# Attention with keys split 3 x 128 + 64, and attention-times-V in four 64x64 tiles, inside a fused attention and FFN kernel

## Chip, cores and metric

The kernel runs on one core of one Trainium2 chip. The metric is the device time of one execution in microseconds (us). Where two kernels are compared, runs from the same chip and the same rounds are used, all of them in the fast state. The experiments ran on four chips, each with the kernel before beside them, so runs of different groups are to be compared by their ratio to it. Times within a run, such as the first `xn`, come from the one execution whose trace was kept. A single core has only one span, so "state" here only says that a run lies within 1.5% of the fastest of its kernel.

Engines are named as in the profile: PE is TensorE's matmuls, PEld its weight loads, DVE is VectorE, ACT is ScalarE, POOL is GpSimd, SP is SyncE. `L179` is line 179 of the kernel. "Half clock" is a stretch in which the trace records a granted TensorE clock of 0.5.

## The reference, cut

```python
# q, k, v: (8, 12, 448, 64) float32       batch, heads, sequence, head size
scores = q @ k.T / sqrt(64)
attn   = maximum(scores, 0) ** 2 / 448
x      = (attn @ v), heads side by side   # (3584, 768)
xn     = x / sqrt(mean(x * x) + 1e-6) * rms_g
g, val = xn @ w_gate, xn @ w_val          # (768, 1536) each
out    = (silu(g) * val) @ w_out          # (1536, 768)
```

## The kernel before

Eight batches of 448 tokens run through attention and FFN. The attention of batch b+1 is woven, piece by piece, into the FFN matmuls of batch b. That makes *stages*: stage b is the FFN of batch b with the attention of batch b+1 inside. By "batch 1's stage" I mean the first of them, in which batch 1's attention runs. The attention of batch 0 has no FFN to hide in and stands alone at the **start**; I take the start to end with the first `xn` instruction of batch 0, which produces the first input of the FFN.

The heads go in pairs (`j`), one head per half of the partitions. The keys are cut into four chunks of 112. For each pair and chunk, two matmuls make scores with keys on partitions, a relu copies them out of PSUM, and a square follows:

```python
NCH = 4                                     # chunks, PC = 112 keys each
def relu_on(b, j, c):   return "dve" if c == 3 and (b or j % 2) else "act"
def square_on(b, j, c): return "pool" if b == 0 and j >= 3 and c == 1 else "dve"

def scores(b, j, c):
    psS = ps_s.tile([P, 2, 512], FP32, ...)  # ps_s has two buffers
    for hh in range(2):                      # two row halves of the array: 64x128 tiles
        nc.tensor.matmul(out=psS[:, hh, :S], lhsT=<chunk c of k>, rhs=<q>, ...)
    ...                                      # relu into r; the square is queued
```

Attention times V is done for two pairs in one *visit*: 16 matmuls of 112 keys onto 64 columns, two heads side by side (`112*64` in the profile):

```python
def attend(b, j):
    psAV = ps_s.tile([P, 2, 512], FP32, ...)
    for jj in range(2):
        for c in range(NCH):
            for hh in range(2):
                nc.tensor.matmul(out=psAV[hh * D : (hh + 1) * D, jj, :S],
                    lhsT=ld["v", b][:, 2 * (j + jj) + hh, c * D : (c + 1) * D],
                    rhs=rsq[b, j + jj, c][:, hh, :], start=(c == 0), stop=(c == NCH - 1))
    ...                                      # ACT copies psAV to xT
```

The order of one batch's attention. Batches 0 and 1 transpose q and k on PE (`transposes`), later ones by DMA. `keep_busy(n)` runs n matmuls of zeros whose result nobody reads; the kernel before has them at the start.

```python
if b < PE_T:                                 # PE_T = 2
    add(0.4, lambda: transposes(b, 0))
for j in range(HP):                          # 6 pairs
    for c in range(NCH):
        if c == 1 and j in (2, 4):
            add(1.6, lambda j=j: attend(b, j - 2))
        add(0.3, lambda j=j, c=c: scores(b, j, c))
        if c == 1 and b < PE_T and j + 1 < HP:
            add(0.4, lambda j=j: transposes(b, j + 1))
        if b == 0 and c % 2:
            add(0.3, lambda: keep_busy(2))
...
add(1.6, lambda: attend(b, HP - 2), flush)
```

## Time and profile before

| | before |
|---|---|
| median time | 468.93 us (468.92 to 469.4) |
| span in the trace, mean granted clock | 467.2 us, 0.997 |
| end of the start (first `xn`) | 39.75 us |
| first relu | 8.70 us |
| first `xn` of batch 0 to first `xn` of batch 7 (seven stages) | 370.13 us |
| the rest, to the end | 57.32 us |

From the overview page: engine busy time and share, then the span in 40 slices of 11.7 us each (each digit is tenths; `PEclk` is the granted TensorE clock), then the chain of waits.

```profile
PE 455.1 (97%) x5440; PEld 297.1 (64%) x5440; DVE 283.0 (61%) x425; ACT 255.6 (55%) x384; POOL 55.7 (12%) x48
...
PE   7889999999999999999999999999999999999995
...
PEclk9999999999999999999999999999999999999998
DMA  9999999799909930499009950428002200020013
...
PE 92%; DVE 4%; ACT 3%; issue 0%; DVEq 0%
```

PE is the limit nearly everywhere. Two other things matter later: the first three PE digits are lower than the rest, which is the start, and `PEclk` stays at 9 there. DMA is busy at 90% or more for almost all of the first 100 us.

The groups that the change touches (line, engine, operation, tiles, shapes, count; busy time, mean ns of one; idle time before them and what ended it):

```profile
L190 ACT ACTIVATE r<-psS 112x896 bf16<-112x896 f32 x147 | 132.7, 920 | 53.5 <-PE psS L179 52.6
...
L179 PE MATMUL psS<-qkT 64*128 64x448 bf16 x384 | 77.7, 350 | 3.8 <-ACT r L190 3.0
...
L203 PE MATMUL psAV<-r,vb 112*64 112x448 bf16 x384 | 41.3, 355 | 0.9 <-DVE r L188 0.5
```

350 ns is the length of one pipelined matmul, not its cost. The cost is the spacing of starts: inside a visit, the pairs of matmuls start every 0.189 us. I call that a *slot*.

The timeline (start, length, engine, line, operation, tiles, count, idle before it and its releaser): first the beginning of the start, then its end, then one visit.

```profile
8.30 0.55 PE L179 MATMUL psS<-qkT 64*128 64x448 bf16 x4 [0.72 <-DVE qkT L160]
8.70 4.96 ACT L190 ACTIVATE r<-psS 112x896 bf16<-112x896 f32 x6 [6.47 <-PE psS L179]
8.78 0.39 PE L155 MATMUL psT<-ident,kb 112*64 112x112 bf16 x8
...
39.75 3.66 DVE L364 SCALAR_TENSOR_TENSOR xn<-xT,g_sb,rstd 128x448 bf16<-128x448 bf16 x6
...
162.02 1.70 PE L203 MATMUL psAV<-r,vb 112*64 112x448 bf16 x16
163.66 0.36 PE L317 MATMUL psP<-xn,wg_sb 64*128 64x448 bf16 x1
```

The scores of pair 0 start at 8.30 us, *before* the transposes of pair 1 (8.78 us), so ACT begins at 8.70 us. The visit's 8 slots last 1.54 us (8 times 0.189, and 0.02 more in the first); with the 0.09 us on entering and 0.10 us on leaving, in which no slot begins, the visit takes 1.73 us from the end of the slot before it to the start of the matmul after it. Every steady visit takes that, within 2 ns.

### The profile page before, as it was taken

The page shows a single profiled execution, that of the slowest core. Times are in us where ns is not written, and L with a number is a line of the kernel's source. Part 1 is how long each engine was busy: PE and PEld are TensorE (multiplying, and loading weights), DVE is VectorE, ACT ScalarE, POOL GpSimd, SP SyncE. Part 2 cuts the span into 40 slices and gives each one's busy share as a digit, 9 for nine tenths or more (in the row PEclk, how much of TensorE's full clock was granted, in tenths as well). Part 3 has the DMA queues.
Part 4 walks back from the last instruction along what each step waited for, and adds up shares of the span by engine and source line. Part 5 has one row for each costly group of instructions (what it writes and reads, how often), then busy time and mean ns, then how long its engine had stood idle before and what let it go on. Part 6 is the DMA issues. An engine that isn't in the chain of part 4 may idle for free.

```text
span 467.2 us, 12220 instructions
## 1 busy us (share of the span) xinstructions
PE 455.1 (97%) x5440; PEld 297.1 (64%) x5440; DVE 283.0 (61%) x425; ACT 255.6 (55%) x384; POOL 55.7 (12%) x48
## 2 busy tenths in 40 slices
PE   7889999999999999999999999999999999999995
PEld 3335556676667666676667666676667766676674
DVE  2876488687664876397666676587565686442210
ACT  3862366666555766475645766565545766532221
POOL 8355100411004000400004000000000000000000
PEclk9999999999999999999999999999999999999998
DMA  9999999799909930499009950428002200020013
GB/s 107 199 204 199 208 169 135 97 201 142 124 6 169 198 65 0 60 204 138 1 1 138 204 95 1 60 84 139 1 1 67 72 2 0 3 80 24 1 38 99
DMA packets 128052, 43.65 MB, mean 93 GB/s; under 512 B 100608, under 2 KB 124416, under 8 KB 128000
## 3 DMA queue, kind: packets, MB, share of 16 engines
q0 software_dynamic: 88944, 23.60, 52.6%
q1 hardware_dynamic: 39056, 19.28, 21.7%
q8 instruction: 42, 0.69, 0.6%
q14 instruction: 10, 0.08, 0.1%
HBM read 47.19 MB, written 11.01 MB: 125 GB/s over the span
## 4 chain that ended last, share of the span: by engine, by line
PE 92%; DVE 4%; ACT 3%; issue 0%; DVEq 0%
PE psP L317 47%; PE psO L317 23%; PE psAV L203 8%; PE psS L179 7%; PE psB L120 2%; PE psSS L317 2%; ACT r L190 2%; DVE r L188 1%; PE psT L155 1%; DVE r L193 1%; DVE xn L364 1%; PE psP L378 1%; DVE rstd L361 1%; ACT xT L214 0%; DVE qkT L160 0%
## 5 line engine op out<-in xcount | busy, mean ns | idle before, releaser
L317 PE MATMUL psP<-xn,wv_sb 64*128 64x448 bf16 x1140 | 236.1, 349 | 0.0
L317 PE MATMUL psP<-xn,wg_sb 64*128 64x448 bf16 x1128 | 234.1, 349 | 0.1
L190 ACT ACTIVATE r<-psS 112x896 bf16<-112x896 f32 x147 | 132.7, 920 | 53.5 <-PE psS L179 52.6
L317 PE MATMUL psO<-wo_sb,hT 64*128 64x256 bf16 x2016 | 141.2, 270 | 0.0
L317 PEld LDWEIGHTS <-hT 64*128 64x128 bf16 x2016 | 103.3, 94 | 30.3 <-issue 3.1
L317 PEld LDWEIGHTS <-wv_sb 64*128 64x128 bf16 x1140 | 94.9, 94 | 41.5 <-issue 2.7
L193 DVE TENSOR_TENSOR r<-r 112x896 bf16<-112x896 bf16 x189 | 113.6, 624 | 9.7 <-ACT r L190 9.0
L317 PEld LDWEIGHTS <-wg_sb 64*128 64x128 bf16 x1128 | 94.5, 94 | 38.5 <-issue 3.2
L393 DVE TENSOR_TENSOR hT<-sil,psP 128x448 bf16<-128x448 bf16 x96 | 59.5, 619 | 81.8 <-PE psP L317 72.8
L388 ACT ACTIVATE sil<-psP 128x448 bf16<-128x448 f32 x96 | 51.9, 541 | 62.1 <-PE psP L317 55.9
L179 PE MATMUL psS<-qkT 64*128 64x448 bf16 x384 | 77.7, 350 | 3.8 <-ACT r L190 3.0
L188 DVE TENSOR_SCALAR r<-psS 112x896 bf16<-112x896 f32 x45 | 49.0, 1089 | 14.6 <-PE psS L179 13.9
L427 ACT COPY ost<-psO 128x256 f32<-128x256 f32 x84 | 30.8, 372 | 42.9 <-PE psO L317 38.8
L214 ACT ACTIVATE xT<-psAV 128x896 bf16<-128x896 f32 x24 | 22.0, 917 | 41.4 <-PE psAV L203 40.2
L203 PE MATMUL psAV<-r,vb 112*64 112x448 bf16 x384 | 41.3, 355 | 0.9 <-DVE r L188 0.5
L361 DVE RECIPROCAL rstd<-rstd 128x448 f32<-128x448 f32 x8 | 23.6, 2952 | 24.4 <-ACT rstd L357 24.4
L179 PEld LDWEIGHTS <-qkT 64*128 64x128 bf16 x384 | 26.5, 94 | 18.5 <-issue 11.0
L203 PEld LDWEIGHTS <-vb 112*64 112x64 bf16 x384 | 20.5, 109 | 19.1 <-issue 8.5
L364 DVE SCALAR_TENSOR_TENSOR xn<-xT,g_sb,rstd 128x448 bf16<-128x448 bf16 x48 | 29.3, 679 | 0.3
L74 POOL DMA_DIRECT2D vb<-in_v_dram x9 | 8.7, 969 | 173.7 <-PE psAV L203 92.0
L216 DVE TENSOR_TENSOR x<-xT 128x896 bf16<-128x896 bf16 x24 | 14.9, 622 | 23.6 <-ACT xT L214 23.6
L76 POOL DMA_DIRECT2D qb<-in_q_dram x6 | 13.8, 2308 | 45.0 <-DMA qkT<-qb 38.4
(35 smaller groups left out, 145.0 us busy)
## 6 DMA issues: line engine op xcount, KB each, us to landing
qb<-in_q_dram POOLq DMA_DIRECT2D x7, 672.0 KB, 13.0
kb<-in_k_dram POOLq DMA_DIRECT2D x7, 672.0 KB, 17.9
vb<-in_v_dram POOLq DMA_DIRECT2D x7, 672.0 KB, 9.0
out_dram<-ost SPq DMA_DIRECT2D x8, 336.0 KB, 3.2
wg_sb<-in_moe_w_gate_dram POOLq DMA_DIRECT2D x4, 576.0 KB, 18.2
wv_sb<-in_moe_w_val_dram POOLq DMA_DIRECT2D x4, 576.0 KB, 19.8
wo_sb<-in_moe_w_out_dram POOLq DMA_DIRECT2D x2, 1152.0 KB, 24.3
out_dram<-ost SPq DMA_DIRECT2D x8, 288.0 KB, 4.5
```

Source lines behind the costliest of these rows:

```text
L179: nc.tensor.matmul(out=psS[:, hh, :S], lhsT=qkT[b][prt, j].rearrange("p t s -> p (t s)")[:, c * PC : c * PC + P], rhs=qkT[b][prt, j, 1, :] ...
L188: nc.vector.tensor_relu(out=r[:], in_=psS[:PC, :, :S])
L190: nc.scalar.activation(out=r[:], in_=psS[:PC, :, :S], func=ACT.Relu)
L193: pending.append(lambda: eng.tensor_tensor(out=r[:], in0=r[:], in1=r[:], op=ALU.mult))
L203: nc.tensor.matmul(out=psAV[hh * D : (hh + 1) * D, jj, :S], lhsT=ld["v", b][:, 2 * (j + jj) + hh, c * D : (c + 1) * D], rhs=rsq[b, j + jj, ...
L214: nc.scalar.mul(out=xT, in_=psAV[:, :, :S], mul=inv_attn)
L317: mm = nc.tensor.matmul(out=self.ps[:, : self.w], lhsT=self.lhsT(i)[prt], rhs=self.rhs(i)[prt], start=(half == 0 and i == 0), stop=(half = ...
L361: nc.vector.reciprocal(out=rstd[:], in_=rstd[:])
L364: nc.vector.scalar_tensor_tensor(out=xn[:, kt, :], in0=xTs[b][:, kt, :], scalar=g_sb[:, kt : kt + 1], in1=rstd[:], op0=ALU.mult, op1=ALU.mult,
L388: nc.scalar.activation(out=s[:], in_=psG[:], func=ACT.Silu)
L393: nc.vector.tensor_tensor(out=hTs[b // 2][:, fb, o : o + S], in0=sil[b, fb][:], in1=psV[:], op=ALU.mult)
L427: nc.scalar.copy(out=ost[:, o : o + w], in_=ps[:, :w])
```

## The change

The intent is to use PE's array fully. A chunk of 112 keys fills 112 of the 128 rows of the largest tile in the profile (128*128, L120's fillers); three chunks of 128 fill them, and the remaining 64 keys of two head pairs share one slot in four 64x64 tiles. Attention times V is cut to 64x64 as well: each chunk of 128 is two halves of 64 keys, so a visit has 28 matmuls, four at a time. Counted in slots, a batch drops from 24 to 21 for the scores and from 24 to 21 for attention times V.

The core of the diff (loading and the split of `scores` cut):

```diff
     def relu_on(b, j, c):
-        return "dve" if c == 3 and (b or j % 2) else "act"
+        return "dve" if c == UH - 1 or (b and j % 2 and c == 2) else "act"
...
+    def rest_scores(b, j):
+        psS = ps_s.tile([P, 2, 512], FP32, name="psS", tag="psS")
+        for hh in range(2):
+            prt = slice(hh * D, (hh + 1) * D)
+            for jj in range(2):
+                nc.tensor.matmul(
+                    out=psS[jj * D : (jj + 1) * D, hh, :S],
+                    lhsT=qkT[b][prt, j + jj, 0, (UH - 1) * P : (UH - 1) * P + D],
+                    rhs=qkT[b][prt, j + jj, 1, :], start=True, stop=True)
...
-    def attend(b, j):
+    def attend(b, j, then=None):
...
+        def run(first):
+            for step in range(UH - (not first)):
+                for prt, jj in ((low, 0), (high, 1)) if first else ((low, 1), (high, 0)):
+                    r, u = pairs[prt][jj][step]
+                    for hh in range(2):
+                        if not first and step == 0:
+                            tc.add_manual_dep(nc.tensor.nop().ins, last[jj, hh].name, behind)
+                        mm = nc.tensor.matmul(out=psAV[hh * D : (hh + 1) * D, jj, :S],
+                            lhsT=v[prt, 2 * (j + jj) + hh, u * D : (u + 1) * D], rhs=r[prt, hh, :], ...)
+                        last[jj, hh] = mm.ins
+        run(True)
+        psR = rest_scores(*then) if then else None
+        run(False)
...
         if b < PE_T:
             add(0.4, lambda: transposes(b, 0))
+            add(0.4, lambda: transposes(b, 1))
+            add(0.3, lambda: rectify(b, 0, UH - 1, rest_scores(b, 0)))
         for j in range(HP):
-            for c in range(NCH):
-                if c == 1 and j in (2, 4):
-                    add(1.6, lambda j=j: attend(b, j - 2))
+            for c in range(UH - 1):
+                if c == 2 and j in (2, 4):
+                    add(1.6, lambda j=j: attend(b, j - 2, (b, j)))
                 add(0.3, lambda j=j, c=c: scores(b, j, c))
-                if c == 1 and b < PE_T and j + 1 < HP:
-                    add(0.4, lambda j=j: transposes(b, j + 1))
-                if b == 0 and c % 2:
-                    add(0.3, lambda: keep_busy(2))
+                if c == 1 and b < PE_T and j + 2 < HP:
+                    add(0.4, lambda j=j: transposes(b, j + 2))
+                if b == 0:
+                    add(0.3, lambda: keep_busy(1))
...
-        add(1.6, lambda: attend(b, HP - 2), flush)
+        add(1.6, lambda: attend(b, HP - 2, (b + 1, 0) if PE_T <= b + 1 < B else None), flush)
...
-            side.insert(len(side) * 2 // 3, (0, lambda b=b: transpose_dma(b + 2)))
+            side.insert(len(side) // 2, (0, lambda b=b: transpose_dma(b + 2)))
```

K and V now come in two loads each, one per half of the partitions, and V's middle 64 rows are loaded into both halves. Because the remaining 64 keys of pairs 0 and 1 share a slot, pair 1 is transposed, and those remaining scores made, before the first ordinary scores.

## The prediction

> **What bounds the kernel.** TensorE: the overview has PE busy 97% at clock 0.997, the chain of waits gives PE 92%. Busy time overstates pipelined matmuls, so I counted slots: in the timeline, pairs of 448-column matmuls start every 0.189 us, of 256 columns every 0.107. At those spacings all matmuls need about 426 of 467 us (estimate). Some 16 us of the rest lie before 41 us, where the first batch's attention is a latency chain (ACT relus of 0.92 us back to back); steady stretches lose only about 2 per 50 us. DVE (61%) and ACT (55%) have room. DMA is nearly saturated until 100 us.

> **What goes, per batch.** Scores: 24 slots become 18 + 3. Attention times V: 24 become 21 (28 matmuls of 64x64 per visit, four at a time, for 16 in twos). Six slots of 0.189 are 1.13 us a batch, 9.1 us for 8, if four tiles run at once. [...] a pair's weight loads and matmuls start 2 to 4 ns apart; each switch into or out of an attention-times-V visit loses about 0.1 us. Visits stay three per batch, so that cost stays. ACT loses 3 relus a batch (0.92 us), DVE 3 squares (0.62); neither is critical outside the start.

> **What is added.**
> - The second half of a visit waits for the first; the remaining scores fill it. Estimate: 0.05 to 0.1 us a visit.
> - A visit now holds both score buffers: the next scores wait for the visit's copy on ACT (0.92 us), with about 1.1 us of other matmuls between: 0 to 0.3 us, twice a batch.
> - V's middle 64 rows are read twice, K comes in two halves: about 2 us more DMA work before batch 2's K lands (73.0 us before).
> - Batch 1's last visit now contains batch 2's scores. Their transposes landed at 86.7 us before; that visit began at 86.1. With the later K I expect 88.5, and PE standing still for about 2 us. Later stages have 10 us of slack.
> - Start: the first scores wait for the second head pairs' loads (landed 8.5 us before, later now): first relu near 11 instead of 8.7 us. Three fewer relus (2.8 us) repay it; projections start about unchanged (40.7 us).

> **Sum.** Six steady stages at 1.13 minus 0.3 give 5 us; batch 1's stage saves 1.1 and loses 2; start about 0. Predicted **464 us**, 8 in 10 between **459** and **469**. Faster by over 2%: 0.13; within 2%: 0.82; slower by over 2%: 0.05.

> **What would show it.**
> - Slots of attention times V in the timeline still 0.189 us with four matmuls each: four-tile step right; 0.25 or more: wrong.
> - PE waits: 1 to 4 us near 87 us on batch 2's DMA transpose: stall step right.
> - PE waits of scores on ACT's copy of the visit: up to 4 us in all.
> - Steady stages each 0.8 to 1 us shorter.
> - First relu near 11 us, first projection at 40 to 42.

> **What would make it wrong.** Four tiles not running at once (visits 0.4 us longer or more: no gain); [...] the start gaining 2 to 3 us because ACT is its limit; transposes landing early enough (then 461) or much later because of seven small K loads (468 or more); more waiting on two score buffers.

The terms add up to about 4 us (5, plus 1.1, minus 2, plus 0 for the start); the figure is 464 us, 4.9 under before. In "a pair's weight loads" a pair is two matmuls in two tiles. The estimate for a visit's inner wait may be read beside the 0.09 to 0.10 us that each switch takes in the trace of before.

## The result

| | before | after |
|---|---|---|
| median time | 468.93 us (4 runs) | 468.48 us (4 runs, 467.72 to 469.04) |
| ratio | | 0.9987, 95% interval 0.997 to 1.0004 |
| span in the trace | 467.2 us | 466.5 us |
| mean granted clock | 0.997 | 0.982 |
| first relu | 8.70 us | 12.43 us |
| end of the start (first `xn`) | 39.75 us | 44.50 us |
| seven stages | 370.13 us | 364.57 us |
| the rest, to the end | 57.32 us | 57.47 us |

A ratio here is the mean time of one kernel's fast runs over that of the other's fast runs of the same rounds, so not quite the ratio of the quoted medians.

The time is the same. But it is not that nothing happened: the seven stages gained 5.56 us and the start lost 4.75 us. The overview page of the changed kernel shows where to look:

```profile
PE 453.6 (97%) x5722; PEld 292.8 (63%) x5722; DVE 274.0 (59%) x403; ACT 234.9 (50%) x360; POOL 80.6 (17%) x97
...
PE   6989999999999999999999999999999999999995
...
PEclk8698999999999999999999999999999999999998
DMA  9999999799907970299209960438002200020013
...
PE 91%; DVE 3%; ACT 2%; DMA 1%; POOL 1%; issue 1%; POOLq 0%
```

The second slice of `PE` reads 9, busier than before, and the second slice of `PEclk` reads 6. PE is busy there because each matmul takes longer: at half clock a filler matmul and the scores after it start 0.48 us apart, just after it 0.30. That is the line to look at: PE's busy share cannot tell useful work from slow work.

The groups:

```profile
L202 ACT ACTIVATE r<-psS 128x896 bf16<-128x896 f32 x123 | 111.1, 918 | 47.5 <-PE psS L212 46.8
...
L212 PE MATMUL psS<-qkT 64*128 64x448 bf16 x288 | 59.3, 358 | 1.9 <-DVE r L200 1.2
...
L258 PE MATMUL psAV<-r,vb 64*64 64x448 bf16 x672 | 43.9, 361 | 1.8 <-POOL r L205 1.2
```

A relu over 128 partitions takes 918 ns, as over 112 (920). ACT has 24 relus fewer.

What PE waited for, in total, times, longest. Before, no wait on a DMA or on POOL was in this list.

```profile
PE psT L177 <- DMA kb<-in_k_dram: 2.4, 1, 2.4
...
PE psS L212 <- DVE r L200: 1.2, 3, 0.5
PE psAV L258 <- POOL r L205: 1.2, 1, 1.2
```

The timeline: the beginning of the start, its last visit, its end, and then the steady visit that answers to the one shown of before.

```profile
9.59 0.64 PE L177 MATMUL psT<-ident,kb 128*64 128x128 bf16 x8 [2.39 <-DMA kb<-in_k_dram]
...
12.43 0.92 ACT L202 ACTIVATE r<-psS 128x896 bf16<-128x896 f32 x1 [10.19 <-PE psS L212]
...
34.10 1.68 POOL L205 TENSOR_TENSOR r<-r 128x896 bf16<-128x896 bf16 x1 [2.93 <-ACT r L202]
34.87 1.39 DVE L205 TENSOR_TENSOR r<-r 128x896 bf16<-128x896 bf16 x1 [0.99 <-ACT r L202]
...
35.84 1.34 PE L258 MATMUL psAV<-r,vb 64*64 64x448 bf16 x10 [1.19 <-POOL r L205]
...
44.50 1.88 DVE L427 SCALAR_TENSOR_TENSOR xn<-xT,g_sb,rstd 128x448 bf16<-128x448 bf16 x3
...
166.31 0.95 PE L258 MATMUL psAV<-r,vb 64*64 64x448 bf16 x16
167.09 0.36 PE L227 MATMUL psS<-qkT 64*64 64x448 bf16 x4
167.32 0.79 PE L258 MATMUL psAV<-r,vb 64*64 64x448 bf16 x12
168.04 0.36 PE L380 MATMUL psP<-xn,wv_sb 64*128 64x448 bf16 x1
```

**The steady part works.** The visit has 4 steps of four matmuls, one slot of remaining scores, and 3 steps of four; the four start within 10 ns of each other (in the second half one starts 0.03 us before the other three) and the steps are 0.189 us apart. Entering and leaving cost 0.09 us each, as before. The pause between the halves is 0.235 us from the start of the scores to the start of the second half, instead of 0.189. With the switches the whole visit takes 1.83 us; it does the attention of two pairs and also the remaining scores of two pairs. Before, that was a visit of 1.73 us and 8 slots of scores; now it is 1.83 us and 6 slots: 1.73 + 8 × 0.189 − 1.83 − 6 × 0.189 = 0.28 us saved per visit, 0.83 us per batch. Measured over the seven stages: 5.56 / 7 = 0.79 us.

**The start is worse.** The transposes of pair 1 now stand ahead of all scores, and their K had not landed (9.45 us; it landed at 8.46 us before, in one load, but at 9.27 in d_mirror below, in one load too). PE is idle for 2.4 us. The first relu comes 3.7 us later. From 9.1 to 19.4 us and again from 36.5 to 39.9 us the trace's clock record has TensorE at half clock; before had none in the start. The windows of the start show it (stretch, its length, then busy us and count for PE, PEld, DVE, ACT and POOL, granted clock, DMA share, GB/s). Before:

```profile
6.00:13.00 7.00, 5.50 (x69) 2.46 (x68) 3.60 (x7) 4.30 (x6) 5.02 (x8) 1.00 1.31 166
13.00:20.00 7.00, 6.07 (x54) 2.63 (x54) 5.86 (x11) 5.12 (x7) 3.24 (x4) 1.00 1.38 201
```

After:

```profile
6.00:13.00 7.00, 4.28 (x43) 1.98 (x42) 2.30 (x3) 0.57 (x1) 6.85 (x10) 0.72 1.36 169
13.00:20.00 7.00, 6.91 (x50) 2.77 (x49) 4.77 (x9) 4.54 (x6) 4.22 (x6) 0.54 1.39 193
...
34.00:41.00 7.00, 5.49 (x42) 1.90 (x42) 2.02 (x2) 1.91 (x4) 6.90 (x8) 0.76 1.33 201
```

In the second row PE is busy 6.91 of 7 us, at a mean clock of 0.54, and ACT gets less to do than before.

### The profile page after: what moved, and what is told of

Read it like the earlier page. It is cut to its first block, busy times and chain, and to the rows that moved or that the text cites. A ratio compares the mean times of both kernels' runs of the same rounds, so it can differ in the third digit from the quotient of the medians.

```text
span 466.5 us, 12798 instructions
## 1 busy us (share of the span) xinstructions
PE 453.6 (97%) x5722; PEld 292.8 (63%) x5722; DVE 274.0 (59%) x403; ACT 234.9 (50%) x360; POOL 80.6 (17%) x97
## 4 chain that ended last, share of the span: by engine, by line
PE 91%; DVE 3%; ACT 2%; DMA 1%; POOL 1%; issue 1%; POOLq 0%
PE psP L380 47%; PE psO L380 23%; PE psAV L258 8%; PE psS L212 6%; PE psSS L380 2%; ACT r L202 2%; PE psB L140 1%; PE psT L177 1%; PE psS L227 1%; DMA kb<-in_k_dram 1%; DVE xn L427 1%; PE psP L441 1%; DVE r L200 1%; DVE r L205 1%; DVE rstd L424 1%
## 5 line engine op out<-in xcount | busy, mean ns | idle before, releaser
L380 PE MATMUL psP<-xn,wv_sb 64*128 64x448 bf16 x1140 | 229.0, 349 | 0.0
L202 ACT ACTIVATE r<-psS 128x896 bf16<-128x896 f32 x123 | 111.1, 918 | 47.5 <-PE psS L212 46.8
L380 PEld LDWEIGHTS <-wv_sb 64*128 64x128 bf16 x1140 | 96.1, 94 | 41.5 <-issue 4.3
L205 DVE TENSOR_TENSOR r<-r 128x896 bf16<-128x896 bf16 x165 | 100.9, 628 | 16.3 <-ACT r L202 15.6
L200 DVE TENSOR_SCALAR r<-psS 128x896 bf16<-128x896 f32 x45 | 49.1, 1090 | 31.7 <-PE psS L227 24.2
L212 PE MATMUL psS<-qkT 64*128 64x448 bf16 x288 | 59.3, 358 | 1.9 <-DVE r L200 1.2
L258 PE MATMUL psAV<-r,vb 64*64 64x448 bf16 x672 | 43.9, 361 | 1.8 <-POOL r L205 1.2
L93 POOL DMA_DIRECT2D kb<-in_k_dram x42 | 33.0, 1008 | 18.7 <-DMA wo_sb<-in_moe_w_out_dram 9.6
L258 PEld LDWEIGHTS <-vb 64*64 64x64 bf16 x672 | 17.3, 106 | 22.3 <-issue 10.3
L212 PEld LDWEIGHTS <-qkT 64*128 64x128 bf16 x288 | 19.8, 94 | 11.4 <-issue 6.2
L140 PE MATMUL psB<-busy_bf,ones_bf 128*128 128x448 bf16 x58 | 17.6, 418 | 1.3 <-DVE busy_bf L135 1.3
## 6 DMA issues: line engine op xcount, KB each, us to landing
wg_sb<-in_moe_w_gate_dram POOLq DMA_DIRECT2D x4, 576.0 KB, 16.5
```

The source lines that it names most:

```text
L93: nc.gpsimd.dma_start(out=to[:, u - u0 : u - u0 + step, h0:h1, :], in_=rows[:, u : u + step])
L200: nc.vector.tensor_relu(out=r[:], in_=psS[:, :, :S])
L202: nc.scalar.activation(out=r[:], in_=psS[:, :, :S], func=ACT.Relu)
L205: pending.append(lambda: eng.tensor_tensor(out=r[:], in0=r[:], in1=r[:], op=ALU.mult))
L212: nc.tensor.matmul(out=psS[:, hh, :S], lhsT=qkT[b][prt, j, 0, c * P : (c + 1) * P], rhs=qkT[b][prt, j, 1, :], start=True, stop=True,)
L258: mm = nc.tensor.matmul(out=psAV[hh * D : (hh + 1) * D, jj, :S], lhsT=v[prt, 2 * (j + jj) + hh, u * D : (u + 1) * D], rhs=r[prt, hh, :], s ...
```

## The experiments

Three theories for the lost 4.75 us stood against each other. CLOCK: the wait on K makes PE idle, the clock falls to half, and the slow stretch is most of the loss. ORDER: the late first relu is the loss, because the chain behind it is bound by ACT whatever the clock. END: the loss is in the start's last visit, where a square on POOL holds things up. All runs gave correct results. "First xn" is read from each run's trace.

| run | what it is | first relu | half clock in the start | first xn | median | ratio to before (95%) |
|---|---|---|---|---|---|---|
| before | | 8.70 | none | 39.75 | 468.93 | |
| after | | 12.43 | 9.1–19.4, 36.5–39.9 | 44.50 | 468.48 | 0.9987 (0.997–1.0004) |
| a_fill | after + filler during the wait | 12.04 | 34.9–38.3 | 41.67 | 465.90 | 0.9928 (0.9913–0.9944) |
| b_first | after, scores first | 8.49 | 16.3–19.7, 33.4–40.2 | 42.94 | 466.52 | 0.9938 (0.9916–0.996) |
| c_square | after, last POOL square to DVE | 12.16 | 9.7–16.5 | 41.55 | 465.68 | 0.9931 (0.9913–0.995) |
| d_mirror | before + pair 1 transposed first | 10.23 | 14.9–18.3 | 42.75 | 471.98 | 1.0056 (1.0038–1.0074) |
| e_fill_square | a + c | 12.20 | none | 40.49 | 465.69 | 0.9921 (0.9903–0.9939) |
| f_order_square | better order + c | 8.72 | 16.8–20.2, 30.4–33.8 | 42.83 | 466.50 | 0.9934 (0.9915–0.9953) |
| g_order_square_wo | f + output weights later | 8.30 | 29.6–33.0 | 40.50 | 465.56 | 0.9917 (0.99–0.9935) |
| k_nopool | after, no POOL squares | 12.32 | 10.6–17.4 | 41.90 | 465.60 | 0.9927 (0.9914–0.994) |
| i_start | order mended, no POOL squares | 7.93 | none | 38.16 | 465.90 | 0.9937 (0.9918–0.9956) |
| j_both | i + batch 2's first remaining scores apart | 7.82 | none | 38.13 | 462.84 | 0.9874 (0.9862–0.9887) |

In the versions of the changed kernel in this table the six stages after batch 1's agree within 0.1 us, except in j, where one stage is 0.4 us longer for its visit of scores. So the first xn and batch 1's stage tell the runs apart. h_two and l_two_wait, which are about the visit, follow at the end.

### a_fill

```diff
             add(0.4, lambda: transposes(b, 0))
+            if b == 0:
+                add(0.4, lambda: keep_busy(12))
             add(0.4, lambda: transposes(b, 1))
```

> The changed kernel with 12 more filler matmuls (2.3 us at full clock) while TensorE waits for the second head pair's K at the start; the wait itself stays. Theory CLOCK (the 2.4 us idle stretch drops TensorE's clock to half from 9.1 to 19.4 us, and the slow stretch is most of what the start lost): no half clock before 20 us, first normalisation (first xn) at 41.5 to 43 us instead of 44.5, total 1.5 to 3 us under the changed kernel, near 466. Rival ORDER (the first relu comes 3.7 us late because three pieces of work and a load stand ahead of it, and the chain after it is bound by ACT, so the clock hardly matters): first relu still near 12, first xn within 0.7 us of 44.5, total within 0.7 us.

First xn came at 41.67 us, 2.8 us earlier, and the total fell by 0.6% (ratio 0.9928 against 0.9987). The first relu hardly moved. Its windows:

```profile
6.00:13.00 7.00, 4.78 (x53) 2.44 (x47) 2.46 (x4) 0.92 (x1) 6.98 (x10) 1.00 1.35 173
13.00:20.00 7.00, 6.75 (x89) 3.30 (x87) 6.20 (x11) 5.96 (x7) 4.09 (x5) 1.00 1.40 199
```

In 13 to 20 us PE began 89 matmuls instead of 50, and ACT was busy 5.96 us instead of 4.54, at full clock. Twelve useless matmuls, put where PE had to wait anyway, buy 2.8 us. That is CLOCK, and it excludes ORDER as the main cause.

### b_first

```diff
-            add(0.4, lambda: transposes(b, 1))
-            add(0.3, lambda: rectify(b, 0, UH - 1, rest_scores(b, 0)))
+            if b:                            # batch 1 as it was
+                add(...)                     # the same two
 ...
+   # batch 0: transposes(0, 1) after the scores of pair 0, chunk 1; the remaining scores after chunk 2;
+   # transposes of pair 2 after (1, 0), 3 after (1, 2), 4 after (2, 1), 5 after (3, 1)
```

> The changed kernel with the first batch's order put back: scores of the first head pair before the second pair's transposes, the remaining scores of pairs 0 and 1 after them; nothing else changed. Both CLOCK and ORDER: first relu at 8.2 to 8.8 us, no half clock before 20 us, first xn 3 to 4.5 us earlier, total 464 to 466. Theory END (the start's loss lies mostly in its last visit, where a square on POOL and the half clock from 36.5 us delay it): no more than 1.5 us gained.

A partial miss. The first relu came at 8.49 us as expected, but first xn only at 42.94. My own order had put pair 3's transposes too early: PE waited 2.0 us at them for K's third load (landed 15.5 us), the clock fell to half at 16.3 us, and again at 33.4 us around the POOL square. The total still came out below the changed kernel. It shows that an early first relu is not enough.

### c_square

```diff
-        return "pool" if b == 0 and j >= 3 and c == 1 else "dve"
+        return "pool" if b == 0 and 3 <= j < 5 and c == 1 else "dve"
```

> The changed kernel with the last of the three squares of batch 0 on POOL moved to DVE (only head pairs 3 and 4 keep theirs). END: the wait of attention times V on POOL (1.2 us) and the half clock from 36.5 to 39.9 us go, first xn 1.5 to 3 us earlier, total near 466. CLOCK and ORDER: a gain of 0.5 to 1.5 us, with the early half clock and the first relu at 12.4 us unchanged.

First xn came at 41.55 us, 2.9 us earlier: END's number. But the gain is not all at the end. The copy of the *first* visit was already 1.3 us earlier than in the changed kernel, long before the square in question, because this run's early half clock lasted 6.8 us (9.7 to 16.5) instead of 10.2. Only the rest, 1.6 us, lies where the edit is: the wait on POOL and the second half clock are both gone. The changed kernel's lines above show how that wait arose: the POOL square takes 1.68 us, and the DVE square that starts beside it takes 1.39 instead of 0.62.

The traces show what the two do to each other: this DVE square began at 34.87 us and ended at 36.26, 0.48 us after the POOL square (35.78). In all the traces kept, 22 DVE squares that began beside a POOL square of 1.68 us took longer than usual (0.78 to 2.05 us), and every one ended 0.48 us after it; six more began in its last 0.1 us and took the usual 0.62.

### d_mirror

The kernel before, with only the order changed:

```diff
             add(0.4, lambda: transposes(b, 0))
+            add(0.4, lambda: transposes(b, 1))
...
-                if c == 1 and b < PE_T and j + 1 < HP:
-                    add(0.4, lambda j=j: transposes(b, j + 1))
+                if c == 1 and b < PE_T and j + 2 < HP:
+                    add(0.4, lambda j=j: transposes(b, j + 2))
```

> The kernel before, with only the second head pair's transposes moved ahead of the first scores (K still in one load, landed 8.5 us). If order and load alone make the loss: first relu near 10 us and first xn 1 to 1.5 us later, total 470 to 470.5. If the clock is what multiplies it: [...] with a drop to half clock it would be 3 us or more.

It lost 3.0 us at first xn and 0.56% in time, more than I expected, and the clock did fall.

```profile
PE psT L155 <- DMA kb<-in_k_dram: 3.5, 2, 2.7
```

PE waited 2.7 us for pair 1's K, and then, since the order looks ahead by two pairs, 0.8 us for K's third load (landed 14.8 us). Half clock followed the second wait, from 14.9 to 18.3 us; the first one, though longer than the changed kernel's 2.4 us, brought none. So in the kernel before, with no 64x64 tile and no chunk of 128, the order alone costs 3.0 us. It is not the same loss as the changed kernel's, which never waited for the third load: the run shows that the order can cost as much, not that it did so there.

### e_fill_square

Both edits, a_fill's and c_square's.

> Both single repairs of the start that gained (fill while waiting for K; last POOL square to DVE) together. If the two losses are separate stretches of the start, they add, but the early half clock that the square's run happened to have shorter counts once: no half clock between 6 and 460 us, first xn near 40 us (44.5 in the changed kernel, 39.75 before), total 463.5 to 464.5. If they are one loss seen twice: no better than 465.5.

No half clock, and first xn at 40.49 us, 4.0 us earlier than the changed kernel. The two losses add, as far as they are separate; what c_square had gained from its shorter half clock counts once. The total missed my range by about 1 us, since something new appeared (PE waits from 80 to 100 us):

```profile
PE psS L227 <- DMA qkT<-qb: 1.3, 1, 1.3
```

That is the stall the prediction named: the last visit of batch 1 wants batch 2's transposes. In the changed kernel that visit began at 89.39 us and the transposes had landed at 86.65, so the late start had hidden it. Here the visit began at 85.37 us and the last transpose landed at 88.13.

### f_order_square and g_order_square_wo

f: as b_first, with pair 2's transposes after (1, 1), pair 3's after (2, 0), 4 after (3, 0), 5 after (4, 0), and c_square's edit. g: f, and the output weights loaded after batch 2's q and k instead of before.

> Order of the start mended (scores of the first pair first, and each later pair's transposes only as early as needed, so that none waits for K's third load) and the last POOL square on DVE. Theory: no idle wait on K over 0.5 us, no half clock, first relu near 8.5 us, first xn 37 to 39 us. Then the first stage begins 2 to 3 us earlier than before, and the stall that the prediction named should appear: the last visit of batch 1 would want batch 2's transposes near 83 to 84 us, they land near 86.5, so TensorE waits 2 to 3 us on the DMA transpose there. Total 463 to 465. If no such stall: 461 to 462.5.

A miss: first xn only at 42.83 us. PE still waited 1.2 us for K's third load, until 16.2 us (half clock 16.8 to 20.2), and then 2.0 us for a relu on DVE. The cause of the second was one of the two POOL squares that I had left: a DVE square beside it took 2.05 us, and the relu stood behind it. Half clock followed (30.4 to 33.8). With so late a start, the stall did not appear.

> As the run before, with the output weights loaded after batch 2's q and k instead of ahead of them. If the stall on batch 2's transposes is real, they land near 80 us now and it goes: 461 to 462.5, 2 us under the run before. If there was none, the same time as that run (within 0.7 us).

Inconclusive. There was no stall to remove, and loading order did not move the transposes: batch 2's K had landed by 62.7 us instead of 73.4, but its transposes then began beside the weight load and landed at 86.07, against 86.38 in f. The 0.2% between f and g goes with one stretch of half clock fewer.

### k_nopool

```diff
-        return "pool" if b == 0 and j >= 3 and c == 1 else "dve"
+        return "dve"
```

> The changed kernel with all three POOL squares of batch 0 on DVE, nothing else. Seen so far: a DVE square beside a POOL square took 1.4 us instead of 0.62, and moving the last one gained 2.9 us at first xn. If only the last one counts: the same as that run, first xn 41 to 42.5 us. If the other two also hold up DVE's relus: first xn 0.5 to 1.5 us earlier still, 40 to 41 us. The early half clock (from about 9 us) stays in both.

First xn at 41.90 us: the same as c_square. In the changed kernel's order only the last of the three POOL squares costs anything. (In f's order another one did.)

### i_start and j_both

i: batch 0 in the order of b_first, with transposes of pairs 1 to 5 after (0, 1), (1, 1), (2, 1), (3, 0), (4, 0), and no squares on POOL. j: i, and

```diff
+        if b == PE_T:
+            add(0.3, lambda: rectify(b, 0, UH - 1, rest_scores(b, 0)))
 ...
-        add(1.6, lambda: attend(b, HP - 2, (b + 1, 0) if PE_T <= b + 1 < B else None), flush)
+        add(1.6, lambda: attend(b, HP - 2, (b + 1, 0) if PE_T < b + 1 < B else None), flush)
```

> The start with its three losses mended at once: order (first pair's scores first, pair 3's transposes after two more scores so that ACT has work while K's third load lands), no squares on POOL. If the start's loss is these waits and the half clock that follows from them: no half clock, no wait on K of TensorE that leaves ACT idle over 1 us, first xn 36.5 to 38.5 us. The last visit of batch 1 then stands near 82 to 83 us and waits 3 to 4 us on batch 2's DMA transposes (landing near 86.5): total 463 to 464.5. If first xn comes no earlier than 40, something else bounds the start.

First xn at 38.16 us, no half clock in the start: 6.3 us earlier than the changed kernel and 1.6 us earlier than before. The start is now shorter than before; the three relus saved would fit that, but the POOL squares that before has are gone too, and no run separates the two. But the total was 465.9 us, not 463 to 464.5. PE's waits from 80 us on:

```profile
PE psS L227 <- DMA qkT<-qb: 3.0, 1, 3.0
```

The stall is 3.0 us as expected, but batch 1's stage became 6.1 us longer (60.70 against 54.63 us in j). The clock again: the stretch after the stall, first i_start, then j_both:

```profile
87.00:94.00 7.00, 6.40 (x54) 3.73 (x56) 2.34 (x3) 2.57 (x3) 5.73 (x7) 0.52 0.63 43
```

```profile
87.00:94.00 7.00, 7.00 (x111) 5.16 (x109) 4.19 (x4) 3.92 (x7) 6.37 (x7) 1.00 1.12 116
```

Half the matmuls in the same 7 us, at a clock of 0.52. In this execution a wait of 3 us cost 6. It was the slowest of i_start's six (467.74 us); the others ran in 464.51 to 467.3 us, at clocks of 0.991 to 0.998, so not every execution pays as much.

> As i_start, and batch 2's first remaining scores no longer inside batch 1's last visit but in a visit of their own at the beginning of batch 2's attention (0.4 us more for that visit). If the wait on batch 2's transposes is what i_start still loses: it is gone and the total is 2 to 3.5 us under i_start, 460.5 to 462. If i_start shows no such wait: 0.3 to 0.5 us slower than it.

The stall and its half clock are gone; j_both is 3.1 us faster than i_start (medians 462.84 and 465.90 us), as expected, though the total is a little above the range I gave. At 462.84 us it is 1.3% faster than before, the best version here.

### h_two and l_two_wait

These ask whether the visit's 1.83 us really comes from four tiles at once. h_two issues all of the low half's matmuls of a pass, then all of the high half's:

```diff
-            for step in range(UH - (not first)):
-                for prt, jj in ((low, 0), (high, 1)) if first else ((low, 1), (high, 0)):
+            for prt, jj in ((low, 0), (high, 1)) if first else ((low, 1), (high, 0)):
+                for step in range(UH - (not first)):
```

> The changed kernel with the matmuls of a visit put in such order that only two tiles of one row half run at a time: the same 28 matmuls in 13 or 14 pairs of slots. If the gain of the steady stages comes from four tiles at once, a visit grows from 1.83 to 3.0 to 3.2 us and the total by 24 times 1.2 to 1.4 us, to 496 to 502. If TensorE already worked on two at a time, nothing changes.

A miss: the visit took 1.89 us, and the time did not change clearly (469.65 us, ratio 1.0008, interval 0.9964 to 1.0052). In this execution K came later (11.07 us) and PE waited 4.9 us for it, so first xn, 46.14 us, says nothing of the visit. The visit's timeline shows the same shape as before the edit:

```profile
115.74 0.97 PE L258 MATMUL psAV<-r,vb 64*64 64x448 bf16 x16
116.52 0.38 PE L227 MATMUL psS<-qkT 64*64 64x448 bf16 x4
```

Sixteen matmuls in four steps, with four starts in each step: two at 0 and two 26 ns later. In the program (the order in `kernel.py`, and in the compiled program) the first eight are all in the low half, which holds two tiles only. So the high half's were begun while earlier ones of the low half had not been: the first of them started 26 ns after the first of the low half, and six of the low half's that stand before it in the program started 0.19 to 0.57 us afterwards. The order of issue does not keep the halves apart; a wait must. l_two_wait adds one:

```diff
+                        if prt is high and step == 0:
+                            other = 0 if first else 1
+                            tc.add_manual_dep(nc.tensor.nop().ins, last[other, hh].name, behind)
```

> The run that put the low row half's matmuls ahead of the high half's changed nothing, because TensorE started the high half's beside them all the same. Now the high half's first matmul of each pass also waits for the low half's last one, so that two tiles at most run at once. If a visit's time comes from four tiles at once: a visit takes 3.1 to 3.4 us instead of 1.83, and the whole 30 to 38 us more than the changed kernel, 498 to 507. If the tiles share something that already held them to two at a time, a visit stays under 2.2 us.

The time rose to 508.09 us and a visit to 3.62 to 3.68 us, a little above both ranges:

```profile
121.55 1.47 PE L261 MATMUL psAV<-r,vb 64*64 64x448 bf16 x10
122.67 0.38 PE L227 MATMUL psS<-qkT 64*64 64x448 bf16 x2
122.83 0.76 PE L261 MATMUL psAV<-r,vb 64*64 64x448 bf16 x6
123.39 0.38 PE L227 MATMUL psS<-qkT 64*64 64x448 bf16 x2
123.61 1.59 PE L261 MATMUL psAV<-r,vb 64*64 64x448 bf16 x12
```

Two tiles at a time cost 1.8 us more per visit. By estimate 14 slots instead of 8 make 6 × 0.189 = 1.13 us of it, and the added waits the remaining 0.7. The slots themselves show it without the waits: in this trace steps of two matmuls are mostly 0.155 to 0.19 us apart, hardly less than the 0.189 of the steps of four in the changed kernel. So the change's steady gain rests on four tiles at once.

## Why the prediction was wrong

Point by point:

- **Four tiles at once: right.** Slots of 0.189 us with four matmuls each; l_two_wait shows what it is worth.
- **The visit's inner wait, 0.05 to 0.1 us: right.** A visit is 1.83 us where 8 slots and the two switches without the wait would be 1.73, as before. The remaining scores do fill it: batch 7's last visit, without them, takes 1.83 us too.
- **Steady stages: right on average.** 0.8 to 1 us each predicted; the six later stages gained 0.24 to 1.42 us, 0.82 on average. The single stages scatter, in the same way in every run of the changed kernel, and why is open. The wait on ACT's copy of the visit was not seen (no such line in PE's waits).
- **Batch 2's transposes: half right.** I expected K about 2 us later, the transposes at 88.5 us and a stall of 2 us. K's last piece landed at 73.9 us (73.0 before, not 75), the transposes at 86.65 us, and the late start hid the stall. It is real, though: 1.3 us in e_fill_square, 3.0 us in i_start. In the changed kernel batch 1's stage gained 0.65 us where I had it lose about 1.
- **The start: wrong, and this is the step that failed.** The prediction said: "Three fewer relus (2.8 us) repay it; projections start about unchanged (40.7 us)." The start's term was put at about 0 and measured +4.75 us at first xn. I had seen that pair 1's loads would hold up the first relu, though not by how much (11 us predicted, 12.43 measured), and I costed that as a shift in a chain bound by ACT. What I left out is that PE stands idle during it and that its clock answers. Then PE, not ACT, sets the pace at half speed for 10 us (from 13 to 20 us PE is busy 6.91 of 7 us at a clock of 0.54, ACT 4.54), and the saved relus buy nothing. The profile of before held the hint: `keep_busy` matmuls throughout the start, in a stretch that PE does not limit. I take them to be there for the clock, and did not draw the consequence.

How the 4.75 us divide can be given only in part, since the pieces interact. Filling the wait gives back 2.8 us (a_fill); the last POOL square with its half clock about 1.6 us more in c_square's trace, and 1.2 us on top of a_fill (41.67 to 40.49 in e_fill_square). What is left, 40.49 against 39.75, is 0.7 us; I put it down to the late first relu, which e_fill_square keeps, though no run shows that alone; i_start, which mends the order too, ends the start at 38.16.

The total that I predicted was a gain of 4.9 us. The seven stages gave 5.56 us, more than the 4 that my terms add up to; the start took 4.75 instead of 0, and that alone undid it.

**Left open:** covered time does not tell what decides a drop: b_first had one after a window of 65%, e_fill_square none after 63%, and l_two_wait one after 84%. A count of work fits better. Count each matmul as its slot (0.189 us per 448 columns, twice that at half clock: the changed kernel's visit has steps of 0.375 us there, from 37.2 to 37.9 us), times the part of a 128x128 tile that its own tile fills. Then all 16 drops in the kept traces, those at the very end left out, follow windows of 35.3% or less; of the other 1794 windows at full clock from 5.5 us on, two stand at 34.5 and 35.5%, and all the rest are above 37%. The three windows named become 35, 38 and 31%: in l_two_wait two quarter tiles together fill half of that. The full clock returned after windows of 72 to 91%, and did not after 51 to 75%. This reading was made after the runs, from the same traces, and no run tests it.

## What to carry to other kernels

Cost an idle stretch of TensorE not by its length but by what the clock does after it: here a wait of 3 us cost 6 in one execution, and covering a wait of 2.4 us with useless matmuls gave back 2.8 us, half of what the change earned in its seven stages. Before moving work ahead of other work on an engine, look at when each of its loads lands (pair 1's K landed at 9.45 us, and PE stood idle for 2.4 us); and when a saving does not show in the total, compare the granted clock by slices first, then stage by stage, because a gain and a loss can cancel almost exactly. Where the wait could not be removed, matmuls of zeros in it were worth their place here.
